# Two groups instead of one by 26 block products, with the weight sums made one group earlier

## The chip, the cores and the metric

The kernel runs on one core of a Trainium2 chip. A core has five engines with their own in-order instruction queues: TensorE (PE in the profile; its weight loads are PEld), VectorE (DVE), ScalarE (ACT), GpSimd (POOL) and SyncE (SP), which here does nothing but issue DMA transfers. [...] All times are device microseconds (us). The metric is the time of one execution on the device; the median of the runs shown is what counts.

## The reference

Two stages follow each other. The first is attention inside chunks of 64 tokens, for 8 batches, 8 heads, 576 tokens and a head size of 64. The second takes its output as `x` of shape (8, 576, 512), mixes it by a Fourier transform over tokens and features, and puts a two-layer perceptron behind it:

```python
mixed = np.real(np.fft.fft(np.fft.fft(x, axis=1), axis=2))
u = x + mixed
un = (u - mean(u)) / np.sqrt(var(u) + 1e-06)
ch = np.maximum(un @ w_ch1, 0.0) @ w_ch2      # 512 -> 2048 -> 512
return u + ch
```

Everything is 32-bit floating point. The two products with `w_ch1` ("up") and `w_ch2` ("down") are by far the largest part.

## The kernel before, in words

**Groups.** The tokens are cut into nine groups of four tiles of 128 tokens, numbered 0 to 8. Groups 0 to 7 belong to one batch each; group 8 holds the middle chunks of all batches. `mlp(g)` runs a group: an up phase, then a down phase. `begin[g]` is the step at which group g starts; a step is one `yield` of these phases, and the other work of the kernel (attention and Fourier mixing of the next batch, weight preparation) is put between the steps by the loop at the end of the kernel. The order on each engine's queue is thus written out by hand: an instruction stands where the loop emits it, and each queue is worked off in that order.

**Three ways to do a down product.** `down_plain` is the direct way. `down_halves` cuts both operands into halves and needs 7 products in place of 8, each of 8 matmuls of 128x128 by 128x256, for two token pairs: 7 x 2 x 8 = 112 matmuls. `down_few` cuts finer and needs 26 products (table `PRODUCTS`, lines 120 to 147), each of 4 such matmuls: 104 matmuls. The price of fewer products is sums. `down_halves` needs sums of activations made by `operands`; `down_few` needs sums of activations made on GpSimd by `sums` (6 in the list `EARLY`, one ahead of the first product, and 21 beside the products), and sums of weight blocks, 23 of them in the list `MADE`. The constant `FEW` (line 1127) says from which group on `down_few` is used: group 8 alone.

**Weights by slab.** From group 1 or 2 on, the weights lie in DRAM, already cut and summed, and come in as slabs through rings. `fetch(1)` loads the slabs of the up phase (256 KB, ring of 10, tile `wa`), `fetch(2)` those of `down_halves` (1 MB, ring of 3, tile `wb`), and `fetch(3)` those of `down_few` (512 KB, tiles `wb`, `xall`, `more`, ring of `NS3` = 11). Each call puts one DMA on SP's queue; that DMA waits until TensorE has read the slab which it overwrites. An up phase has 28 turns of 4 matmuls, one slab each, and a `fetch(1)` behind each turn. In `down_few` there is a `fetch(3)` behind each product.

**Making the weight sums.** `make_rest` (line 1088) is a generator that the loop advances a step at a time, from step `ready_at[NG - 3]` on, which lies four steps into the down phase of group 6. It does the 23 sums of `MADE` in two halves of 128x512 each. For each half it loads eight blocks from DRAM (line 1104), makes the sums on GpSimd (line 1113), and stores the 19 that are wanted to the DRAM tile `s3` (line 1120). Loads and stores go over SP's queue. The list `spare` holds the buffers: 14 pieces of 128x512, taken from tiles that the attention no longer needs. A sum takes a buffer from its front. A store is issued once more than three made sums stand behind it, and its buffer goes back to `spare`; whoever writes to it next waits until that store has landed.

**The order around it.** At step `begin[8] + 2`, two steps into the up phase of group 8, the loop adds five slabs to the ring and issues all eleven `fetch(3)` at once. Each DMA on SP also waits for the DMA issued eight places before it, on SP or ACT, since eight completion semaphores are used in turn. `store` (line 1020) writes finished tiles to the output.

Of the kernel before, what the change touches and what calls it, by code (L numbers as in the profile page):

```python
# [8 lines left out]
FP32 = mybir.dt.float32  # L9
# [7 lines left out]
def kernel(  # L17
# [32 lines left out]
    nc = tc.nc  # L50
# [16 lines left out]
    G = 2 * NM  # L67
# [4 lines left out]
    one_p = ctx.enter_context(tc.tile_pool(name="one", bufs=1))  # L72
    two_p = ctx.enter_context(tc.tile_pool(name="two", bufs=2))
    three_p = ctx.enter_context(tc.tile_pool(name="three", bufs=3))
# [77 lines left out]
        "s24=s10-sb22", "s22=w-s10", "s25=w+s4", "s1=b21-s4", "s17=b21+b41", "s18=b12+b32", "s12=s18-s17", "s6=b42-s18",  # L152
    )
    STORED = tuple(text.split("=")[0] for text in MADE if text[0] == "s")
    NR2, NS3 = len(PRODUCTS), 11
    s3 = dram.tile([len(STORED), 128, Z3], FP32, name="s3")
    slab3 = [wb[:, i * Z3:(i + 1) * Z3].rearrange("p (m e) -> p m e", m=4) for i in range(6)]

# [922 lines left out]
    def block_of(name):  # L1081

        if name[0] == "s":
            return s3[STORED.index(name)]
        o, k = (2, "dw".index(name)) if name in "dw" else ({"b1": 0, "b2": 0, "b3": 4 + "12".index(name[2]), "b4": 4 + "12".index(name[2])}[name[:2]], (int(name[1]) - 1) % 2)
        return s2[o, :, k * Z3:(k + 1) * Z3]

    def make_rest():

        z, spare = Z3 // 2, []
        for i in range(4):
            spare.append(xall[:, 2 * G:2 * G + 4, :].rearrange("p a f -> p (a f)")[:, i * z:(i + 1) * z])
        for tag, n in (("q", 2), ("k", 2), ("zf", 2), ("two", 1), ("qT", 1), ("kT", 1), ("pT", 1)):
            t = one_p.tile([128, n * z], FP32, tag=tag, name="part")
            spare += [t[:, i * z:(i + 1) * z] for i in range(n)]
        last = {x: i for i, text in enumerate(MADE) for x in text.replace("=", "-").replace("+", "-").split("-")}
        for half in range(2):
            part = slice(half * z, (half + 1) * z)  # L1100
            where, behind = {}, []
            for name in ("b31", "b41", "b42", "b11", "b32", "d", "w", "b21"):
                where[name] = spare.pop(0)
                nc.sync.dma_start(out=where[name], in_=block_of(name)[:, part])
                if half and name in ("b41", "b11", "d"):
                    yield
            yield
            for i, text in enumerate(MADE):
                name = text.split("=")[0]
                to = spare.pop(0)  # L1110
                name, *used, op = parsed(text)
                in0, in1 = (where[x] for x in used)
                nc.gpsimd.tensor_tensor(out=to, in0=in0, in1=in1, op=op)
                where[name] = to
                if name in STORED:
                    behind.append(name)
                done_with = [x for x in (*used, name) if last[x] == i]
                while behind and (len(behind) > 3 or i == len(MADE) - 1):
                    old = behind.pop(0)
                    nc.sync.dma_start(out=block_of(old)[:, part], in_=where[old])  # L1120
                    if last[old] <= i and old not in done_with:
                        done_with.append(old)
                spare += [where[x] for x in done_with if x not in behind]
                if i % 2:
                    yield

    FEW = NG - 1
    first_of = {1: 2, 2: 1}
    n_slab = {1: 0, 2: 0, 3: 0}

    def fetch(which):
        i = n_slab[which]
# [276 lines left out]
    with tc.manual_schedule():  # L1409
# [74 lines left out]
        for g in range(NG):  # L1484
            for _ in mlp(g):
# [29 lines left out]
                if t == begin[1] - 1:  # L1515
                    for _ in conv2:
                        pass
                if t == ready_at[NG - 3]:
                    rest_ = make_rest()
                    next(rest_)  # L1520
                if t > ready_at[NG - 3] + 4:
                    next(rest_, None)
                if t == begin[FEW] + 2:
                    more = [xall[:, 2 * G:2 * G + 4, :].rearrange("p a f -> p (a f)")[:, i * Z3:(i + 1) * Z3] for i in range(2)]
                    more += [one_p.tile([128, Z3], FP32, tag=tag, name="more") for tag in ("q", "k", "zf")]
                    slab3.extend(a.rearrange("p (m e) -> p m e", m=4) for a in more)
                    for _ in range(NS3):
                        fetch(3)
                if begin[1] <= t < begin[1] + KF // 2:
                    for _ in range(3):  # L1530
                        next(conv1, None)
# [55 lines left out]
```

## Time and profile before

Three runs of the kernel took 1081.45, 1081.10 and 1078.39 us; the median is 1081.1 us.

| | |
|---|---|
| profiled execution, its own time | 1078.96 us |
| its span, first to last instruction | 1076.9 us |
| granted TensorE clock | 0.998 |
| up phase of group 7 | 875.28 to 925.33 us of the span |
| down phase of group 7 (`down_halves`) | 925.33 to 975.43 us |
| up phase of group 8 | 975.43 to 1026.41 us |
| down phase of group 8 (`down_few`) | 1026.41 to 1071.32 us |

In a row of the profile, "L1377 PE MATMUL dn<-wb,h" is the line of the kernel, the engine, the operation, and the tile written from the tiles read. "<-DVE" names the engine that ended a wait. A line with "SPq" is about SP's queue, which issues DMAs. The chain of work is followed back from the last instruction; in it TensorE's weight loads are counted with its matmuls, so "x8" of a product is 4 matmuls with their 4 loads.

### The profile page before, as it was taken

The numbers are of one execution on the slowest core, as the hardware profiler recorded it, in microseconds if no ns is written. First come the engines' busy times: TensorE is split into PE (matmuls) and PEld (weight loads), VectorE is DVE, ScalarE is ACT, GpSimd is POOL, SyncE is SP. The second block draws the span as 40 slices with busy tenths as digits, with TensorE's granted clock in tenths as the row PEclk, the third lists the DMA queues.
The fourth block names the chain that finished last, engine by engine and source line by source line (L and its number), as shares of the span: only waits on it lengthen the run. The fifth ranks groups of instructions, "written<-read, shape, count | busy, mean of one in ns | idle before, by whom it ended". The sixth has DMA issues, their size and how long they took to land.

```text
span 1076.9 us, 19916 instructions
## 1 busy us (share of the span) xinstructions
PE 1053.0 (98%) x7402; PEld 837.3 (78%) x7402; DVE 585.0 (54%) x1271; ACT 310.3 (29%) x730; POOL 406.1 (38%) x531
## 2 busy tenths in 40 slices
PE   8999989999999999999999999999999999999997
PEld 6645445446888888888888888888888888888786
DVE  4898985324567465664565554745564435433331
ACT  4688563212113411322032312331233012101200
POOL 4311017573515140344134321624061837850281
PEclk9999999999999999999999999999999999999999
DMA  8767466598467546883678256945653569957563
GB/s 176 240 184 214 122 190 210 162 299 292 153 193 224 161 155 181 231 238 118 189 210 229 99 183 199 260 129 189 208 158 110 196 211 317 337 174 241 186 225 107
DMA packets 159293, 212.71 MB, mean 198 GB/s; under 512 B 69308, under 2 KB 106172, under 8 KB 152926
## 3 DMA queue, kind: packets, MB, share of 16 engines
q1 hardware_dynamic: 155548, 208.04, 63.0%
q10 hardware_dynamic: 3330, 2.76, 1.1%
q8 instruction: 59, 0.97, 0.4%
q0 software_dynamic: 320, 0.66, 0.3%
q14 instruction: 36, 0.29, 0.1%
HBM read 177.31 MB, written 34.08 MB: 196 GB/s over the span
## 4 chain that ended last, share of the span: by engine, by line
PE 77%; DMA 6%; DVE 5%; issue 3%; POOL 3%; ACT 3%; SPq 3%; POOLq 0%; DVEq 0%; ACTq 0%
PE pb L1313 18%; PE pa L1262 16%; PE pa L1313 14%; PE pb L1262 12%; PE dn L1377 4%; PE up L1195 2%; PE pt L397 2%; DMA xall<-in_moe_w_ch_dram 2%; PE mix L838 2%; DMA wa<-s 2%; PE z L719 1%; PE xp L498 1%; SPq L263 1%; PE up L1175 1%; PE sc L448 1%
## 5 line engine op out<-in xcount | busy, mean ns | idle before, releaser
L1262 PE MATMUL pa<-unT,wa 128*128 128x256 f32 x672 | 159.9, 381 | 1.6 <-DVE wa L1270 1.6
L1262 PEld LDWEIGHTS pa<-unT,wa 128*128 128x128 f32 x672 | 126.3, 190 | 19.5 <-DVE wa L1270 2.1
L1262 PE MATMUL pb<-wa 128*128 128x256 f32 x448 | 106.7, 381 | 2.6 <-DMA wa<-s 2.6
L1313 PE MATMUL pa<-wb,h 128*128 128x256 f32 x448 | 101.5, 380 | 0.0
L1313 PE MATMUL pb<-wb,h 128*128 128x256 f32 x448 | 100.7, 379 | 0.0
L1262 PEld LDWEIGHTS pb<-wa 128*128 128x128 f32 x448 | 84.2, 190 | 14.8 <-issue 2.8
L1313 PEld LDWEIGHTS pa<-wb,h 128*128 128x128 f32 x448 | 83.9, 190 | 11.3
L1313 PEld LDWEIGHTS pb<-wb,h 128*128 128x128 f32 x448 | 84.1, 190 | 10.9
L1149 POOL TENSOR_TENSOR h<-h 128x256 f32<-128x256 f32 x56 | 47.0, 850 | 96.2 <-DVE wb L1147 93.4
L555 POOL COPY xall<-xall 1x512 f32<-1x512 f32 x28 | 17.8, 636 | 147.9 <-DVE xall L515 120.4
L1268 DVE TENSOR_TENSOR wa<-pb,wa 128x256 f32<-128x256 f32 x56 | 23.7, 424 | 73.0 <-ACT wa L1267 73.0
L1216 PE MATMUL dn<-wb,h 128*128 128x512 f32 x128 | 58.9, 609 | 0.0
L1267 ACT COPY wa<-pa 128x256 f32<-128x256 f32 x56 | 20.8, 372 | 126.8 <-PE pa L1262 126.8
L1195 PE MATMUL up<-unT,wa 128*128 128x512 f32 x128 | 56.8, 596 | 0.0
L1262 PE MATMUL pa<-wa 128*128 128x256 f32 x224 | 53.9, 384 | 0.8 <-DMA wa<-s 0.8
L1262 PE MATMUL pb<-unT,wa 128*128 128x256 f32 x224 | 53.0, 379 | 0.0
L1313 PE MATMUL pb<-wb,yall 128*128 128x256 f32 x224 | 51.2, 382 | 0.0
L1313 PE MATMUL pb<-wb 128*128 128x256 f32 x224 | 50.7, 379 | 0.0
L1313 PE MATMUL pa<-wb,yall 128*128 128x256 f32 x224 | 50.5, 379 | 0.0
L1276 ACT ACTIVATE h<-pa 128x256 f32<-128x256 f32 x56 | 21.5, 383 | 100.7 <-PE pa L1262 99.8
L1175 PE MATMUL up<-unT,wa 128*128 128x512 f32 x108 | 49.4, 598 | 0.0
L1262 PEld LDWEIGHTS pa<-wa 128*128 128x128 f32 x224 | 41.7, 190 | 7.2 <-ACT wa L1267 1.1
(287 smaller groups left out, 1955.7 us busy)
## 6 DMA issues: line engine op xcount, KB each, us to landing
wb<-s SPq DMA_DIRECT2D x49, 1024.0 KB
wa<-s SPq DMA_DIRECT2D x196, 256.0 KB
xall<-in_moe_w_ch_dram SPq DMA_DIRECT2D x22, 512.0 KB
q<-in_q_dram SPq DMA_DIRECT2D x96, 112.0 KB
k<-in_k_dram SPq DMA_DIRECT2D x96, 112.0 KB
wb<-s SPq DMA_DIRECT2D x16, 512.0 KB
v<-in_v_dram SPq DMA_DIRECT2D x124, 64.0 KB
s<-part SPq DMA_DIRECT2D x30, 256.0 KB
```

The lines of the kernel that those rows point to most:

```text
L397: nc.tensor.transpose(pt[:, j, :], src(j), ident)
L838: nc.tensor.matmul(out=mix[:, cols], lhsT=zt[:, T], rhs=tab, start=(T == 0), stop=(T == 3), skip_group_check=True,)
L1149: nc.gpsimd.tensor_tensor(out=h1[:, m, hi], in0=h1[:, m, lo], in1=h1[:, m, hi], op=ALU.subtract)
L1175: nc.tensor.matmul(out=up, lhsT=w1[:, kk, m * 128:(m + 1) * 128], rhs=unT[:, kk], start=(kk == 0), stop=(kk == KD - 1), skip_group_check=True,
L1195: nc.tensor.matmul(out=up, lhsT=w1[:, kk, m * 128:(m + 1) * 128], rhs=unT[:, kk], start=(kk == 0), stop=(kk == KD - 1),)
L1216: nc.tensor.matmul(out=dn, lhsT=h1[:, m, s * 128:(s + 1) * 128], rhs=w2[:, m, :], start=(m == 0), stop=(m == KF - 1),)
L1262: nc.tensor.matmul(out=dst, lhsT=w[:, kk, r], rhs=rhs[o][:, kk], start=(o in (0, 1) and kk == 0), stop=(kk == 1), skip_group_check=True,)
L1267: nc.scalar.copy(a, dst)
L1268: nc.vector.tensor_tensor(out=b, in0=pbs[r][:, 0], in1=a, op=ALU.add)
L1276: nc.scalar.activation(out=h1[:, m, lo], in_=dst, func=ACTF.Relu)
L1313: nc.tensor.matmul(out=dst, lhsT=lhs[:, m], rhs=w[:, m], start=(o in (0, 2) and m == 0), stop=(m == HF - 1), skip_group_check=True,)
L1377: nc.tensor.matmul(out=dst, lhsT=lhs[:, m], rhs=w[:, m], start=(fresh and not half and m == 0), stop=(m == 3), skip_group_check=True,)
```

## The change

`FEW` becomes `NG - 2`, so groups 7 and 8 both run `down_few`; group 7's up phase makes the `EARLY` sums in place of `operands`. For that the weight sums are needed one group earlier, and `make_rest` is rewritten. It has 21 pieces of buffer in place of 14: two each of the tiles `ex` and `pm` and three of `y` are added. It loads 13 of its 16 blocks at once, the other three as buffers come free (`take`). Four of the 23 sums of each half go to VectorE in place of GpSimd: every fourth, unless it reads one of the two sums just before it. The loop advances it at every step without the pause of four steps, and at step `begin[7] + 12` runs what is left of it. There the ring gets two slabs more, eight in all in place of eleven, and two `fetch(3)` are issued in each of the last four steps of group 7's up phase. The slabs of group 8 then follow through the ring behind group 7's products. No DMAs of `fetch(2)` are issued for group 7.

```diff
-    NR2, NS3 = len(PRODUCTS), 11
+    NR2, NS3 = len(PRODUCTS), 8
...
-        for tag, n in (("q", 2), ("k", 2), ("zf", 2), ("two", 1), ("qT", 1), ("kT", 1), ("pT", 1)):
-            t = one_p.tile([128, n * z], FP32, tag=tag, name="part")
+        for pool, tag, n in (
+            (one_p, "q", 2), (one_p, "k", 2), (one_p, "zf", 2), (one_p, "two", 1), (one_p, "qT", 1), (one_p, "kT", 1),
+            (one_p, "pT", 1), (two_p, "ex", 1), (two_p, "ex", 1), (two_p, "pm", 1), (two_p, "pm", 1),
+            (three_p, "y", 1), (three_p, "y", 1), (three_p, "y", 1),
+        ):
+            t = pool.tile([128, n * z], FP32, tag=tag, name="part")
             spare += [t[:, i * z:(i + 1) * z] for i in range(n)]
...
+        def take(keep):
+            while wanted and len(spare) > keep:
+                half, name = wanted.pop(0)
+                places[half][name] = spare.pop(0)
+                nc.sync.dma_start(out=places[half][name], in_=block_of(name)[:, half * z:(half + 1) * z])
+
+        take(8)
+        yield
         for half in range(2):
-            part = slice(half * z, (half + 1) * z)
-            where, behind = {}, []
-            for name in ("b31", "b41", "b42", "b11", "b32", "d", "w", "b21"):
-                where[name] = spare.pop(0)
-                nc.sync.dma_start(out=where[name], in_=block_of(name)[:, part])
-                if half and name in ("b41", "b11", "d"):
-                    yield
-            yield
+            part, where, behind = slice(half * z, (half + 1) * z), places[half], []
             for i, text in enumerate(MADE):
...
-                nc.gpsimd.tensor_tensor(out=to, in0=in0, in1=in1, op=op)
+                eng = nc.vector if i % 4 == 3 and not {MADE[i - 1].split("=")[0], MADE[i - 2].split("=")[0]} & set(used) else nc.gpsimd
+                eng.tensor_tensor(out=to, in0=in0, in1=in1, op=op)
...
                 spare += [where[x] for x in done_with if x not in behind]
+                take(7)
                 if i % 2:
                     yield
-    FEW = NG - 1
+    FEW = NG - 2
...
-                if t == ready_at[NG - 3]:
+                if t == ready_at[FEW - 1]:
                     rest_ = make_rest()
-                    next(rest_)
-                if t > ready_at[NG - 3] + 4:
+                if t >= ready_at[FEW - 1]:
                     next(rest_, None)
-                if t == begin[FEW] + 2:
-                    more = [xall[:, 2 * G:2 * G + 4, :].rearrange("p a f -> p (a f)")[:, i * Z3:(i + 1) * Z3] for i in range(2)]
-                    more += [one_p.tile([128, Z3], FP32, tag=tag, name="more") for tag in ("q", "k", "zf")]
-                    slab3.extend(a.rearrange("p (m e) -> p m e", m=4) for a in more)
-                    for _ in range(NS3):
-                        fetch(3)
+                if t == begin[FEW] + 2 * HF - 4:
+                    for _ in rest_:
+                        pass
+                    slab3.extend(
+                        one_p.tile([128, Z3], FP32, tag=tag, name="more").rearrange("p (m e) -> p m e", m=4)
+                        for tag in ("q", "k")
+                    )
+                if begin[FEW] + 2 * HF - 4 <= t < begin[FEW] + 2 * HF:
+                    fetch(3)
+                    fetch(3)
```

More of the change, by code (lines that the diff above doesn't have):

```diff
@@ L1094, in make_rest @@
             spare.append(xall[:, 2 * G:2 * G + 4, :].rearrange("p a f -> p (a f)")[:, i * z:(i + 1) * z])
-        for tag, n in (("q", 2), ("k", 2), ("zf", 2), ("two", 1), ("qT", 1), ("kT", 1), ("pT", 1)):
-            t = one_p.tile([128, n * z], FP32, tag=tag, name="part")
+        for pool, tag, n in (
[4 more added lines that the diff above has]
+            t = pool.tile([128, n * z], FP32, tag=tag, name="part")
             spare += [t[:, i * z:(i + 1) * z] for i in range(n)]
         last = {x: i for i, text in enumerate(MADE) for x in text.replace("=", "-").replace("+", "-").split("-")}
-        for half in range(2):
-            part = slice(half * z, (half + 1) * z)
-            where, behind = {}, []
-            for name in ("b31", "b41", "b42", "b11", "b32", "d", "w", "b21"):
-                where[name] = spare.pop(0)
-                nc.sync.dma_start(out=where[name], in_=block_of(name)[:, part])
-                if half and name in ("b41", "b11", "d"):
-                    yield
-            yield
+        places = [{}, {}]
+        wanted = [(half, name) for half in range(2) for name in ("b31", "b41", "b42", "b11", "b32", "d", "w", "b21")]
+        def take(keep):
[5 more added lines that the diff above has]
+        yield
+        for half in range(2):
+            part, where, behind = slice(half * z, (half + 1) * z), places[half], []
             for i, text in enumerate(MADE):
-                name = text.split("=")[0]
                 to = spare.pop(0)
```

## The prediction

> **What bounds the kernel now.** The page first: one engine is nearly always busy.
>
> ```profile
> span 1076.9 us, 19916 instructions
> PE 1053.0 (98%) x7402; PEld 837.3 (78%) x7402; DVE 585.0 (54%) x1271; ACT 310.3 (29%) x730; POOL 406.1 (38%) x531
> ```
>
> TensorE is the bound, so I count matmuls and TensorE's gaps in the stages that the change touches. These are the phases of groups 7 and 8, in the busy times by stretch (span, PE, PEld, DVE, ACT, POOL, clock, DMA share, GB/s):
>
> ```profile
> 875.28:925.33 50.05, 49.05 (x226) 42.33 (x225) 24.87 (x52) 13.55 (x31) 34.07 (x29) 1.00 0.89 307
> 925.33:975.43 50.10, 50.10 (x241) 44.14 (x241) 15.80 (x30) 2.45 (x6) 31.29 (x29) 1.00 0.61 204
> 975.43:1026.41 50.98, 48.59 (x225) 42.49 (x225) 16.95 (x40) 13.88 (x31) 7.99 (x7) 1.00 0.61 216
> 1026.41:1071.32 44.91, 44.89 (x208) 39.19 (x207) 12.09 (x30) 0.54 (x2) 26.85 (x22) 1.00 0.58 189
> ```
>
> Rows 1 and 3 (up phases) have idle TensorE time; rows 2 and 4 (down phases) have none. The last row is the form that the change extends: 104 matmuls in 44.91 us, without a gap. The chain of waits gives the cadence, and where the gaps come from:
>
> ```profile
> 980.61 1.74 PE pb L1262 x8
> ...
> 984.16 7.75 DMA wb<-s
> ...
> 991.97 9.89 DMA wa<-s
> ...
> 1002.00 1.97 PE pb L1262 x8
> ```
>
> 4 matmuls take 1.727 us, so one takes 0.432. An up phase is 112 matmuls, 48.36 us; group 8's took 50.98: 2.62 lost, because eleven slabs (5.8 MB) issued at 982.7 to 991 stand ahead of its own weights. Group 7's took 50.05: 1.69 lost. There SP's queue waits for the weight sums, and the sums for buffers (waits of SP's queue, then of GpSimd):
>
> ```profile
> SPq L1120 <- POOL part L1113: 22.6, 16, 5.9
> POOL part L1113 <- DMA s<-part: 23.0, 5, 15.5
> ```
>
> [...] from 984 to 1008 us the DMA share is 0.97 to 1.03 while the weights wait behind the slabs. Saturated 6 us stretches moved 346 to 420 GB/s, most near 380. [...] the 128x256 VectorE sum of line 1148, both inputs in SBUF, took 846 ns on average, that of line 1268 with one input in PSUM 424 ns.
>
> **The change, part by part.**
>
> *Matmuls.* Group 7's down phase goes from 112 to 104: 8 x 0.432 = **-3.45 us**. Its 16 transposes for group 8 (4 x 0.44) stay, so 50.10 becomes 46.65. The last turn of group 8's tiles now has two products (3.45 us) behind it; one 0.69 us copy and four 0.42 us sums on VectorE must end there. They fit.
>
> *The batch of eleven slabs goes.* Group 8's slabs come one by one behind group 7's products: **-2.62 us** in group 8's up phase.
>
> *Activation sums.* Group 7 loses `operands` (16 VectorE sums at 0.69 and 0.85: 12 us; 8 GpSimd sums) and gains 28 GpSimd sums at 1.27, which GpSimd does beside 104 matmuls in group 8 without a TensorE gap. Nothing on the path.
>
> *Sums on VectorE.* 8 x 128x512. The nearest row, line 855, has 0.75 us[...]; I take 8, less than `operands` gave back. Cost nothing, covered by VectorE's idle half; but the evictions of TensorE's results queue behind each, and TensorE behind those. Each sum waits for the store that frees its buffer, so I checked each: the second half's first is due at about 885 with its buffer stored near 884.5, the next at 890 against 888.6, the last two have 7 us or more.
>
> *Slab ring 11 to 8.* A slab is fetched when one product ends and needed 7 products (12.1 us) later; 0.524 MB per 1.727 us is 303 GB/s, below 380. In the trace's own 104-matmul phase the stretches ran at 206 to 315 GB/s with no gap. Nothing, while the ring starts full.
>
> *Weight sums earlier.* This decides. I follow three queues, with these rates: a GpSimd sum 1.27 us; a 256 KB store 4 us from issue to landing (issued 870.4, GpSimd released 875.1; 882.6 to 886.3), 5 where DMA is saturated; one 256 KB transfer per 0.62 to 0.70 us at saturation.
>
> 1. Loads go at 838.3 as now, 13 of them, to 846.5. GpSimd starts at 844.5 instead of 850.5, since its first two sums stand ahead of group 6's output sums. SP's fetches for group 6 wait for TensorE until 846.4 and 853.7; the third, at 861.1, was group 7's and is gone, so four stores go out at 854 to 855.5. GpSimd's next seven sums then end by 867; the trace of before had it idle from 859.6 to 875.1.
> 2. Output stores of group 6 hold SP until 865.0, 868.9, 874.1 and 876.8, as now. The first half's sums end near 882, against 905.
> 3. From 877 on DMA is full. To the end of group 7's up phase SP has 27 stores, 3 loads and 28 `fetch(1)` of 262 KB and 8 slabs of 524 KB: 19.4 MB. The first `fetch(1)` goes at 882.4 (886.05 before). Each has 10 turns from freeing to need, 17 us; I find 5 us or more left for every one. So up 7 has no reason to lose its 1.69 us; as the queue is fuller than before I credit half: **-0.85 us**.
> 4. GpSimd's second half, with the six `EARLY` sums between, is held by buffer stores to about 891.7 and then runs its last 18 instructions back to back: 18 x 1.27 = 22.9, so the last sum ends at 915 and the last store is issued there. `make_rest` is due to be through at step 12 of 16, 911.6; 3 us late.
> 5. The slabs follow from 915.3 at 1.34 us each, with seven `fetch(1)` between. Slab 0 lands near 919.3 (needed at 923.7), slab 4 at 927.4 (930.6), slab 7 at 932.8 (935.8), slab 10 at 937.5 (941). About 3 us to spare; no stall.
>
> *Tail.* The last product ends the same way; 5.6 us stay.
>
> Sum: -3.45 - 2.62 - 0.85 = **-6.9 us**: span 1070.0, the profiled execution 1078.96 - 6.9 = 1072.0. That execution lies 2.1 below the median of the runs (1081.1, which would give 1074.2); I take **1073**.
>
> **The rivals.**
>
> *A: the slabs come late and eat the gain.* By bytes: 19.4 MB from 877 until slab 7 is needed at 935.8 asks for 330 GB/s. At 350 nothing changes. At 300 it takes 64.7 us and the stall is 6 us; down 7 then asks for 303 and does not recover. For it: the up phase of group 7 already had a share of 0.89, at 307 GB/s. Against: that mean holds the waits of SP for sums; the full stretches in it had 358 to 404. Time: 1073 + 6 = 1079, within 0.3% (about what a measurement of this kernel can tell from no change).
>
> *B: the buffer loop runs late, slower than before.* Place: the second half's sums wait in a chain for stores (eight waits, about three sums apart), and SP, in order, has `fetch(1)` and later the slabs behind those stores. Price: each us of landing beyond my 4 to 5 is paid up to eight times in the last sum. A last store at 918 costs nothing, 926 cancels the gain (stall 8), beyond 929 the kernel is over 0.3% slower; that is landing at 6 to 6.5 us. At 931: stall 13, 1073 + 13 = 1086. VectorE's sums, waiting for the same stores, would hold evictions in the same case. For it: before, the second half took 911.1 to 952.6, 1.8 us a sum. Against: 11 us of that were other GpSimd work, and the first half's stores had the fetches of TensorE's pace between them. At that pace, from 883, the end is near 921: stall 3, 1076.
>
> *C: the change does not do what it says.* In the order of the built program group 7's down phase has 104 matmuls and the slabs stand where the text puts them. Left out.
>
> **How the numbers follow.** Likeliest, no stall over 4 us: 0.74, with 1069.5 to 1077. A: 0.12, counted as the same. B beyond its point: 0.14, slower. Faster 0.74, same 0.12, slower 0.14. The range goes from 1068 (all 7.8 us gained, from the lowest run, 1078.39 - 7.8 = 1070.6, less 2.6 for the spread of the runs) to 1083: it leaves out most of B.
>
> **What would show it.** Group 7's down phase at 46.6 us with 104 matmuls of `dn`; group 8's up phase at 48.4 with no wait for `wa`; group 7's up phase at 48.4 to 49.5. Last sum of `make_rest` at 913 to 919 on GpSimd. Wrong if TensorE's first products of group 7's down phase wait for `wb` or `more`, if a `wa` wait of some us stands in its up phase, or if evictions there wait behind a VectorE sum.

## The result: slower by 0.4%, where 0.7% faster was predicted

The changed kernel took 1084.01 us (median of 8 runs, 1082.51 to 1085.91), the kernel before, beside it on the same chip, 1080.72 us (8 runs). The ratio is 1.0036, with a 95% interval of 1.0024 to 1.0048. The prediction was 1073; 1084 lies outside its range as well. The profiled execution took 1082.51 us. Its page, first lines:

```profile
span 1080.5 us, 19943 instructions
PE 1053.7 (98%) x7386; PEld 837.2 (77%) x7386; DVE 593.0 (55%) x1281; ACT 310.1 (29%) x728; POOL 417.3 (39%) x533
```

Eight matmuls are gone (two records each: 7402 to 7386), yet TensorE is busy as long as before. Where the time is shows in the busy times by stretch. These are group 6's down phase, group 7's up and down, group 8's up and down (columns as in the prediction: length, then PE, PEld, DVE, ACT, POOL, clock, DMA share, GB/s):

```profile
822.94:880.17 57.23, 55.28 (x265) 48.40 (x265) 32.91 (x55) 7.85 (x29) 33.93 (x28) 0.97 0.56 188
880.17:932.81 52.64, 50.14 (x225) 43.50 (x224) 22.86 (x45) 13.64 (x31) 39.89 (x31) 0.97 0.88 297
932.81:981.33 48.52, 47.23 (x226) 41.10 (x225) 18.20 (x44) 1.87 (x4) 27.10 (x22) 1.00 0.92 352
981.33:1030.20 48.87, 48.58 (x225) 42.50 (x225) 16.96 (x40) 13.89 (x31) 8.01 (x7) 1.00 0.46 149
1030.20:1075.11 44.91, 44.90 (x209) 39.20 (x207) 12.09 (x30) 0.54 (x2) 26.82 (x22) 1.00 0.66 224
```

Group 6's down phase, whose own products the change does not touch, was this in the kernel before:

```profile
821.87:875.28 53.41, 53.41 (x266) 47.28 (x265) 25.37 (x52) 7.83 (x29) 23.87 (x22) 1.00 0.53 177
```

So the 10.5 us between the predicted span, 1070.0, and 1080.5 come together like this:

| stage | predicted, us | measured, us | more, us |
|---|---|---|---|
| before these phases (the change does nothing there) | 821.87 | 822.94 | 1.07 |
| group 6, down | 53.41 | 57.23 | 3.82 |
| group 7, up (50.05 - 0.85) | 49.20 | 52.64 | 3.44 |
| group 7, down | 46.65 | 48.52 | 1.87 |
| group 8, up | 48.36 | 48.87 | 0.51 |
| group 8, down | 44.91 | 44.91 | 0.00 |
| tail | 5.6 | 5.4 | -0.2 |

Only group 8's two phases came as predicted. The chain of waits in group 8's up phase no longer holds slabs; the load that it still passes costs TensorE 0.3 us there (48.87 less 48.58), not 2.4:

```profile
986.51 1.73 PE pb L1271 x8
...
988.57 10.18 DMA wa<-s
```

TensorE's waits from 840 to 990 us (by line and tile, what ended them, total us, times, longest):

```profile
PE pa L1271 <- DVE h L1287: 2.5, 1, 2.5
PE pt L397 <- DVE un L994: 1.9, 1, 1.9
PE dn L1386 <- DMA more<-s: 1.3, 1, 1.3
```

These are 5.7 us. Behind each of the first two the clock was halved for 3.413 us, which costs 1.7 us each time. Three stretches around the wait that ended at 869.2 us show it in the clock's column (third from the end): 1.00 in the stretch with the wait, 0.50 in the next, in which TensorE was busy throughout and has 9 matmul records, and 1.00 again in the third, with 17. The last section has the other such stretches.

```profile
866.66:870.08 3.42, 1.48 (x9) 1.05 (x8) 2.94 (x4) 0.00 (x0) 3.34 (x3) 1.00 0.00 0
870.08:873.49 3.41, 3.41 (x9) 2.71 (x9) 0.96 (x3) 0.00 (x0) 0.13 (x1) 0.50 0.31 79
873.49:876.90 3.41, 3.41 (x17) 2.98 (x16) 2.13 (x6) 0.00 (x0) 0.00 (x0) 1.00 0.71 166
```

**Why the normalised tile was late.** VectorE's queue in group 6's down phase, changed kernel (start, us, line, operation):

```profile
862.48 0.97 DVE L1015 TENSOR_TENSOR wa<-unT 128x256 f32<-128x256 f32 x1
863.48 1.38 DVE L1016 TENSOR_TENSOR wa<-unT,wa 128x256 f32<-128x256 f32 x1
864.78 1.48 DVE L1017 TENSOR_TENSOR unT<-unT 128x256 f32<-128x256 f32 x1
866.19 1.48 DVE L1018 TENSOR_TENSOR wa<-unT,wa 128x256 f32<-128x256 f32 x1
867.60 1.48 DVE L994 TENSOR_SCALAR un<-xall,st,rstd 128x512 f32<-128x512 f32 x1
869.00 0.41 DVE L1339 TENSOR_TENSOR wb<-pb,wb 128x256 f32<-128x256 f32 x1
...
873.82 0.42 DVE L1016 TENSOR_TENSOR wa<-unT,wa 128x256 f32<-128x256 f32 x1
```

The same instructions in the kernel before:

```profile
861.86 0.42 DVE L1016 TENSOR_TENSOR wa<-unT,wa 128x256 f32<-128x256 f32 x1
862.20 0.42 DVE L1017 TENSOR_TENSOR unT<-unT 128x256 f32<-128x256 f32 x1
862.54 0.42 DVE L1018 TENSOR_TENSOR wa<-unT,wa 128x256 f32<-128x256 f32 x1
862.87 0.54 DVE L994 TENSOR_SCALAR un<-xall,st,rstd 128x512 f32<-128x512 f32 x1
864.59 0.42 DVE L1330 TENSOR_TENSOR wb<-pb,wb 128x256 f32<-128x256 f32 x1 [1.18 <-PE pb L1313]
```

Of the first five, all but line 1015 take 1.4 to 1.5 us in place of 0.4 to 0.5, so 0.9 to 1.1 us longer, beside GpSimd sums of 1.27 us each. In the changed kernel GpSimd sums weights back to back from 857.9 to 870.2; in the kernel before it was idle from 859.6 to 875.1. The changed kernel has its own comparison: at 873.8 us, with GpSimd idle, line 1016 takes 0.42 us again. Counted from the start of the phase, the tile of line 994 is ready at 46.1 us in place of 41.5, and TensorE waits 1.95 us for it.

**Why the weight sums were late.** A sum on GpSimd ended at 863.2 (first line); it was stored from SyncE's queue at 871.2, 8 us later, and the sum that needs its buffer began at 880.3, 9 us after that. GpSimd's queue, then SyncE's, then what SyncE had waited for from 855 to 882 us:

```profile
861.88 1.29 POOL L1121 TENSOR_TENSOR xall<-part 128x512 f32<-128x512 f32 x1
...
880.31 1.27 POOL L1121 TENSOR_TENSOR xall<-part 128x512 f32<-128x512 f32 x1 [10.10 <-DMA s<-xall]
```

```profile
869.43 1.10 SPq L1027 DMA_DIRECT2D out_dram<-wb  x2
870.63 0.46 SPq L1128 DMA_DIRECT2D s<-part  x1
871.18 2.03 SPq L1128 DMA_DIRECT2D s<-xall  x1
```

```profile
SPq L1027 <- DVE wb L1339: 11.5, 1, 11.5
```

SyncE stood 11.5 us at an output store of group 6 (line 1027), with the weight stores behind it. Until 865.6 it stood there for TensorE's product, and from then to 869.4 for VectorE, whose last sum for that tile (line 1339, at 869.00) had to go behind the five slowed instructions. In the kernel before, that sum (line 1330, at 864.59) followed its product at once.

Then the landing. In the trace each of these weight stores has 16 counts on its semaphore. Of the store issued at 871.2, 14 came by 877.5 and the last two at 878.8 and 880.2; the sum began at 880.3. Two output stores of the LO kind stood ahead of it, issued at 869.4 and 870.0.

GpSimd's waits for such stores came to 10.1 and 6.1 us, both in the first half of the weight sums. That half ended at 893.1; the prediction had 882. The second half had no further wait for a store and kept the delay: its last sum ended at 926.4, and the first slab was issued at 926.8; the prediction had 915 and 915.3.

### The profile page after: what moved, and what is told of

It reads as the page before. It is cut to its first block, busy times and chain, and to the rows that moved or that the text cites. A ratio compares the mean times of both kernels' runs of the same rounds, so it can differ in the third digit from the quotient of the medians.

```text
span 1080.5 us, 19943 instructions
## 1 busy us (share of the span) xinstructions
PE 1053.7 (98%) x7386; PEld 837.2 (77%) x7386; DVE 593.0 (55%) x1281; ACT 310.1 (29%) x728; POOL 417.3 (39%) x533
## 4 chain that ended last, share of the span: by engine, by line
PE 74%; DMA 8%; DVE 5%; issue 4%; POOL 3%; ACT 3%; SPq 2%; DVEq 0%; POOLq 0%; ACTq 0%
PE pa L1271 16%; PE pb L1322 15%; PE pb L1271 12%; PE pa L1322 12%; PE dn L1386 7%; PE up L1204 2%; PE pt L397 2%; DMA xall<-in_moe_w_ch_dram 2%; DMA v<-in_v_dram 2%; PE mix L838 2%; PE z L719 1%; DMA wa<-s 1%; PE xp L498 1%; SPq L263 1%; PE up L1184 1%
## 5 line engine op out<-in xcount | busy, mean ns | idle before, releaser
L1271 PEld LDWEIGHTS pb<-wa 128*128 128x128 f32 x448 | 84.4, 190 | 11.5
L1322 PE MATMUL pa<-wb,h 128*128 128x256 f32 x384 | 87.2, 380 | 0.0
L1322 PE MATMUL pb<-wb,h 128*128 128x256 f32 x384 | 86.8, 381 | 0.0
L1322 PEld LDWEIGHTS pb<-wb,h 128*128 128x128 f32 x384 | 72.5, 191 | 9.5
L1322 PEld LDWEIGHTS pa<-wb,h 128*128 128x128 f32 x384 | 71.8, 190 | 9.7
L1158 POOL TENSOR_TENSOR h<-h 128x256 f32<-128x256 f32 x48 | 40.6, 855 | 93.6 <-DVE wb L1156 91.2
L1172 POOL TENSOR_TENSOR h<-h 128x512 f32<-128x512 f32 x36 | 45.1, 1267 | 27.2 <-ACT h L1291 22.5
L1386 PE MATMUL dn<-wb,h 128*128 128x256 f32 x224 | 50.5, 379 | 0.0
L855 POOL TENSOR_TENSOR xall<-y,xall 128x513 f32<-128x513 f32 x14 | 21.4, 1526 | 68.3 <-DVE y L849 68.3
```

The costliest lines, as they stand in the source:

```text
L1158: nc.gpsimd.tensor_tensor(out=h1[:, m, hi], in0=h1[:, m, lo], in1=h1[:, m, hi], op=ALU.subtract)
L1172: nc.gpsimd.tensor_tensor(out=out_, in0=a, in1=b, op=op)
L1271: nc.tensor.matmul(out=dst, lhsT=w[:, kk, r], rhs=rhs[o][:, kk], start=(o in (0, 1) and kk == 0), stop=(kk == 1), skip_group_check=True,)
L1322: nc.tensor.matmul(out=dst, lhsT=lhs[:, m], rhs=w[:, m], start=(o in (0, 2) and m == 0), stop=(m == HF - 1), skip_group_check=True,)
L1386: nc.tensor.matmul(out=dst, lhsT=lhs[:, m], rhs=w[:, m], start=(fresh and not half and m == 0), stop=(m == 3), skip_group_check=True,)
```

## Experiments

Each ratio is to the kernel before, run beside it. The edits are made to the changed kernel, or to the one named. Executions of one kernel spread over some 5 us, so single profiles are read for waits, and medians and ratios for time.

**Is it the sums, or the products?** The first run leaves out the weight sums with their loads and stores; the products then read other blocks that lie in DRAM, so its results are not those of the reference.

```diff
-            return s3[STORED.index(name)]
+            o = STORED.index(name)
+            return s2[o % 7, :, o // 7 % 2 * Z3:(o // 7 % 2 + 1) * Z3]
...
-                if t == ready_at[FEW - 1]:
-                    rest_ = make_rest()
...
```

> The changed kernel without `make_rest`: none of the 46 sums, their 16 loads and 38 stores; the slabs of the 26 products are read from blocks that lie in DRAM anyway, so the products are of the wrong weights. Two groups of 26 products and the ring of eight stay. Theory V (only the making of the sums costs): both gaps and the wait for the slabs go, 1080.7 - 3.45 - 2.6 - 1.7 = 1073. A rival P (26 products beside group 8's preparation, or a ring of eight, cost time themselves): above 1076.

1072.13 us, ratio 0.9922 (0.9894 to 0.9950), from five executions of 1071.7 to 1078.5 us. The profiled one is the slowest; it lost its time ahead of these phases. The phases themselves, group 7 up and down:

```profile
882.59:930.93 48.34, 48.34 (x225) 42.55 (x224) 16.96 (x40) 13.71 (x31) 7.83 (x7) 1.00 0.62 194
930.93:977.59 46.66, 46.66 (x226) 41.09 (x225) 18.56 (x44) 1.87 (x4) 27.13 (x22) 1.00 0.94 335
```

There is no idle TensorE time in them, nor in group 8's up phase, which took 48.34 us. The products, the ring and the missing batch of slabs are worth what was predicted; what is lost is lost through the weight sums, their loads and stores included. The counterpart keeps the sums where they are and gives group 7 its old down phase:

```diff
-    FEW = NG - 2
+    FEW = NG - 1
...
-                if t == ready_at[FEW - 1]:
+                if t == ready_at[FEW - 2]:
...
```

> The changed kernel with 26 products in group 8 alone: the weight sums are made early and with the new buffers as in the changed kernel, group 7 has its 112 matmuls, and the eight slabs are issued in the last four steps of group 8's up phase. Theory V: it pays for the gap in group 6's down phase (3.7) and for a VectorE sum's wait in group 7's up phase (up to 4.2), and gains 2.6 in group 8's up phase, where no batch of eleven slabs stands in the way: 1082 to 1086. Rival P: 1080.7 - 2.6 = 1078.

1089.17 us, ratio 1.0078 (1.0053 to 1.0102): 8.4 us slower than the kernel before, and more than the 1082 to 1086 expected. So the early sums cost time with no new product to be late for. The 8.4 us are not their price in the changed kernel, though: here group 7's up phase still makes `operands` beside them and waits 5.8 us in the profile, and group 8's up phase gains its 2.6 us.

**VectorE's share.**

```diff
-                eng = nc.vector if i % 4 == 3 and not {MADE[i - 1].split("=")[0], MADE[i - 2].split("=")[0]} & set(used) else nc.gpsimd
+                eng = nc.gpsimd
```

> The changed kernel with all 46 weight sums on GpSimd, none on VectorE. Theory V: the wait of 3.4 us of a VectorE sum for a buffer's store in group 7's up phase, and TensorE's gap of 2.5 us behind it with its 1.7 us of slow clock, are gone (-4.2); but GpSimd has eight sums more (8 x 1.27), the last sum ends some 5 us later and TensorE waits about 4 us more for the first slabs of group 7's down phase: 1082 to 1085, with the gap moved. Rival D: -0 in the up phase, +5 at the slabs: 1088.

1087.18 us, ratio 1.0055 (1.0034 to 1.0076): worse, above the 1082 to 1085 expected and near the 1088 of the rival. TensorE's waits:

```profile
PE dn L1386 <- DMA wb<-s: 6.4, 1, 6.4
PE pt L397 <- DVE un L994: 2.1, 1, 2.1
```

The wait for the normalised tile is there without any weight sum on VectorE, so it comes from GpSimd's sums. And the wait in the up phase, gone here, came back as a wait of 6.4 us for slabs, not of 4: GpSimd's last sum ended at 930.0.

**The normalised tile.** In `down_halves` the normalisations go ahead of the operand sums of `combined` (lines 1015 to 1018), so that TensorE's next tile does not stand behind them.

```diff
-                        if k == 5 + 2 * j and j >= 2:
+                    for j in range(2, G):
+                        if k == 5 + 2 * j:
```

> The changed kernel, with the normalising of the next group's tile (VectorE) emitted ahead of that group's four operand sums in `down_halves`. Theory V (VectorE is held by GpSimd's sums[...], the normalised tile of group 7 comes late, TensorE waits 1.95 us, and the clock then runs at half speed for 3.41 us, which costs 1.71): the gap near 868 us goes, group 6's down phase is back at 53.4 us, and the time falls by about 3.7 us to 1080.3. Rival D (the DMA engines are full and everything later is set by them): the down phase gets shorter but the first products of group 7 wait longer for their slabs; 1083 to 1084 stays.

1081.30 us, ratio 1.0012 (0.9999 to 1.0024), 2.6 us less than the change. TensorE's waits from 840 to 990 us:

```profile
PE pa L1271 <- DVE h L1287: 3.1, 1, 3.1
PE pa L1271 <- ACT wa L1276: 1.5, 1, 1.5
```

The wait at line 397 is gone and nothing took its place in group 6, whose down phase takes 53.5 us again. Its half clock is gone too, so 3.8 us are gained there, and part of it is lost in group 7's up phase, where the waits are 4.6 us and not 2.5. The rival, that the DMA engines set everything, asked for 1083 to 1084 us and a longer wait for the first slabs, which the list does not have. The first wait left is an eviction behind a weight sum on VectorE, which waits for a GpSimd sum, which waits for a stored buffer.

**What a wait costs.** The kernel before, with 11 idle additions on VectorE ahead of the same normalisation:

```diff
+                            if g == 6 and j == 3:
+                                for _ in range(11):
+                                    nc.vector.tensor_tensor(out=warm, in0=warm, in1=warm, op=ALU.add)
```

> The kernel before with 11 additions on a tile that nothing reads (about 0.46 us each) ahead of the last normalisation of group 6's down phase, so that VectorE is late there as in the changed kernel. Theory (a gap of some 2 us in TensorE's work is what group 6's down phase cost): 2 us slower than before if the gap alone counts, 3.7 if the clock is halved for 3.4 us after it as in the changed kernel's profile. Rival (other work hides it): no change.

1085.25 against 1081.21 us, ratio 1.0039 (1.0025 to 1.0054): 4.2 us. Its profile has a wait of 2.7 us there and no half clock behind it:

```profile
PE pt L397 <- DVE un L994: 2.7, 1, 2.7
```

The lower end of the interval, 2.7, is the wait alone. Half clock in other executions does not explain the rest: the granted clock is on record for each, and its mean is 0.9967 in the 11 executions of this kernel and 0.9967 in the 20 of the kernel before. What the rest is stays open.

**Landing: the output stores on ScalarE.** On top of the run with the normalisations first; then the same edit on the kernel before.

```diff
-                nc.sync.dma_start(out=to, in_=o[r0:r0 + CH])
+                nc.scalar.dma_start(out=to, in_=o[r0:r0 + CH])
```

> The change with the normalisations ahead of the combined products, and the output stores of the LO kind issued from ScalarE instead of SyncE. Theory (the buffer stores of the weight sums land 7 to 9 us after issue because they queue behind the output stores[...]): they land in 3 to 4 us now, GpSimd's waits of 9.6 and 5.4 us at its sums shrink below 3 each, VectorE's wait of 4.0 us at line 1121 and TensorE's gaps of 3.1 and 1.5 us in group 7's up phase go, with the stretch at half clock; about 1077 us. Rival (the landing is set by the load on the engines, not by the queue): waits and gaps stay, about 1081 us.

> The kernel before with only the LO output stores on ScalarE's queue. Both theories: it has no early weight sums that wait for stores near an output store, so about 1080.5 us, at most 1.5 us faster[...]. It prices that edit alone, so that the run beside it is read rightly.

1089.26 us, ratio 1.0069 (1.0046 to 1.0093), and 1085.86 us, ratio 1.0042 (1.0021 to 1.0064). The edit itself costs 4.6 us, which neither theory had. The second run's profile shows most of it lost in the first groups: a matmul at 168 us of the span comes 1.6 us later than the same one in the kernel before, one at 210 us 6.9 later. An issue took ScalarE 0.5 us at the median there. So the first run's time tells little of its question. What its profile does tell is that GpSimd still waited 9.8 us for a store: a queue of its own for the LO stores did not bring the buffers back in 4 us. Without VectorE's sums in the second half:

```diff
-                eng = nc.vector if i % 4 == 3 and not {...
+                eng = nc.vector if half == 0 and i % 4 == 3 and not {...
```

> The run with normalisations first and LO stores on ScalarE, and VectorE's share of the weight sums kept to the first half; the second half's go to GpSimd. If VectorE's wait for a stored buffer is what still holds TensorE in group 7's up phase, that gap goes, and GpSimd's last sum ends some 5 us later: 1076 to 1078 us while the slabs still come in time; with the slabs late by up to 3 us, 1080.

1089.55 us, ratio 1.0075 (1.0055 to 1.0094). The wait behind the weight sum went, 4.9 us of slab waits came, and 3.4 for a copy on ScalarE: missed.

**Landing: stores moved or left out.** On top of the run with the normalisations first, two stores of group 6 are held back, or left out.

```diff
-                    store(low, olow)
+                    if g == FEW - 1:
+                        held.append((low, olow))
+                    else:
+                        store(low, olow)
...
+                if t - begin[FEW] in (5, 9):
+                    store(*held.pop(0))
```

> The change with the normalisations first, and group 6's two LO output stores, which nothing waits for before group 7's down phase, issued 6 and 10 steps into group 7's up phase (some 19 and 31 us in) and not at 868 and 878 us. Theory (the weight sums' buffers come back late[...]): the first store lands in 4 to 5 us and not 9, GpSimd's first wait falls from 9.6 to under 5 us, VectorE's sum near 892 us no longer waits, TensorE's gaps of 3.1 and 1.5 us and the half clock go: about 1076 us. Rival (the landing is late whatever the output stores do): as with the normalisations first alone, 1081 us.

> The change with the normalisations first, and group 6's LO output stores left out, so two tiles of that group are never written to the output; all else is computed. It is the bound of moving them: by the theory every weight store of the first half lands in 4 to 5 us, GpSimd's waits of 9.6 and 5.4 us together fall below 5, and TensorE's gaps in group 7's up phase go: 1074 to 1077 us. By the rival, 1081 us with the same waits.

These texts name the stores wrongly: `low` is the first two of the group's four tiles, one of the LO and one of the HI kind. 1083.86 us, ratio 1.0024 (1.0012 to 1.0035), and with the two left out 1079.01 us, ratio 0.9981 (0.9968 to 0.9994); 1076, and 1074 to 1077, were expected. The landing did change: in the second run the 16 counts of a weight store came between 867.3 and 868.0, and those of the next between 868.7 and 868.8. But GpSimd's wait did not; SyncE's and GpSimd's waits of that run:

```profile
SPq L1027 <- DVE wb L1347: 9.1, 1, 9.1
```

```profile
POOL part L1121 <- DVE h L1290: 11.7, 1, 11.7
```

SyncE now stood 9.1 us at the third tile's output store. (The second row's name misleads: by its semaphore that sum waited for a weight store, issued at 878.1, 8.5 us after its data was ready and just behind the third tile's LO store; its last two counts came at 886.0 and 886.7. VectorE's instruction happened to end then.) So of these 17 us half is landing and half is the queue, and the queue became the next suspect.

**The queue.** Again with the normalisations first: all of group 6's output stores on ScalarE, in this group alone:

```diff
-                nc.sync.dma_start(out=to, in_=o[r0:r0 + CH])
+                (nc.scalar if n in groups[FEW - 1] else nc.sync).dma_start(out=to, in_=o[r0:r0 + CH])
...
-                    eng = nc.scalar if r else nc.sync
+                    eng = nc.scalar if r or n in groups[FEW - 1] else nc.sync
```

> The change with the normalisations first, and all of group 6's output stores (of that group alone) issued from ScalarE. Theory (in SyncE's queue the weight sums' stores stand behind output stores that wait for TensorE's evictions, so a buffer whose sum was done at 870 is stored only at 882): the weight stores are issued within 1 us of their sums, GpSimd's waits of 9.6 and 5.4 us fall below 5 together, VectorE's wait of 4.0 us near 892 and TensorE's gap of 3.1 us behind it go: 1075 to 1078 us; ScalarE's eight issues, some 0.5 us each, may cost up to 1.5 us at the head of group 7. Rival (the landing alone is late): waits and time as with the normalisations first alone, 1081 us.

1083.20 us, ratio 1.0030 (1.0018 to 1.0042). GpSimd's waits for stores fell from 15.0 to 7.8 us and VectorE's went, but TensorE lost 5.5 us to ScalarE, more than the 1.5 allowed for:

```profile
PE pa L1271 <- ACT wa L1276: 5.5, 1, 5.5
```

Then SyncE's output stores of group 6 held back to the first four steps of group 7:

```diff
+        hold = n in groups[FEW - 1] and not now
+        if hold:
+            held.append((n, o))
...
+                if begin[FEW] < t <= begin[FEW] + 4:
+                    store(*held.pop(0), now=True)
```

> The same aim on SyncE's own queue: group 6's output stores that SyncE issues are held back to the first four steps of group 7's up phase (about 881 to 893 us), when their data has long been there, so that nothing waits behind them. By the queue theory the sums run on without a wait up to about 881, GpSimd's last sum ends near 915 and no gap follows in group 7's up phase: 1074 to 1077 us. By the landing theory the four stores only move the late landings some 10 us on: 1080 us or more.

1078.71 us, ratio 0.9982 (0.9965 to 1.0000): 5.8 us less than the change, and short of the 1074 to 1077 expected. GpSimd's waits, then all of TensorE's from 840 to 990 us:

```profile
POOL xall L1130 <- DMA s<-xall: 4.2, 1, 4.2
POOL part L1130 <- DMA s<-part: 3.8, 3, 1.6
```

```profile
PE dn L1396 <- DMA wb<-s: 4.2, 1, 4.2
```

From the first weight sum to the end of the last it took 73.3 us, against 80.1 in the changed kernel and 70.5 in the prediction. SyncE still stood 6.3 us, to 880.0, now at a weight store whose own sum is one of VectorE's and went behind the four sums of `combined`, each slowed to 1.3 to 1.5 us. So holding the output stores back does not empty the queue of everything that waits. No wait is left in group 7's up phase but the one at its end, for the first slab. The clock is at half for 6.8 us from 930.9 on; 1.9 us of that lie in the wait itself, so 2.5 us are lost (16 matmul records took 6.12 us there and 3.62 at full clock; group 7's down phase takes 49.16 us, not 46.65). The held stores without the other edit:

> The changed kernel with group 6's output stores held back and nothing else altered: the edit that is worth 2.6 us on top of the normalisations first, here by itself. If the two causes add, 1084.0 - 2.6 = 1081.4 us, and TensorE's gap at the turning of the normalised tile (1.95 us in the changed kernel) stays or grows, since GpSimd runs on beside VectorE; if the queue in SyncE was behind that gap too, it goes and the time is 1079 us.

1079.30 us, ratio 0.9987 (0.9975 to 0.9999), 5.3 us less than the change. That is the time expected if the wait for the normalised tile went with the queue, but the wait is still there. The two causes do not add: 2.6 and 5.3 singly, 5.8 together. In this profile the wait for the tile comes without a half clock (the granted clock is 1.00 over 800 to 1070 us and 0.999 over all):

```profile
PE dn L1395 <- DMA wb<-s: 2.2, 2, 1.9
PE pt L397 <- DVE un L994: 2.0, 1, 2.0
PE dn L1395 <- DMA more<-s: 1.2, 1, 1.2
```

**The slabs.** On top of both edits: two slabs loaded early, then six between the weight stores, then the same with the last two at the end of the phase.

```diff
-                if begin[FEW] + 2 * HF - 4 <= t < begin[FEW] + 2 * HF:
+                if t == begin[FEW] + 2 * HF - 7 or begin[FEW] + 2 * HF - 4 <= t < begin[FEW] + 2 * HF - 1:
```

> The normalisations first, group 6's output stores held back, and the first two slabs of group 7's down phase (stored blocks that no weight sum makes) loaded five steps earlier, ahead of the last weight stores in SyncE's queue. If the slabs behind the last stores are what TensorE's 4.2 us at the head of that down phase waits for, that gap goes, with the half clock behind it: 1078.7 - 4.2 = 1074.5 us, or down to 1073 in runs that lost the clock too. If the third slab is as late, 1077 to 1078 us.

> The normalisations first, group 6's output stores held back, and the first six slabs of group 7's down phase loaded between the last weight stores, each some five stores after its own block was stored, and not behind all of them. If the slabs' place in SyncE's queue is the third cause, TensorE's wait of 2.7 us for the third slab and the 6.8 us at half clock behind it (3.4 us lost) go: 1079.0 - 2.7 - 3.4 = 1073 us, the predicted time; 1075 to 1076 if only some runs lost the clock before. If another load is late in its place, 1077 to 1079 us.

> As the run with six slabs early, but the seventh and eighth (into the two buffers that the last weight sums were in) loaded at the end of the up phase and not 3 steps before it, so that SyncE doesn't stand 6.6 us at 928 to 936 waiting for the last weight stores with seven loads behind it. If that standing is what made that run 3 us slower than the one with two slabs early: 1074 to 1077 us, no wait of TensorE for a slab over 1 us. If the loads are late in any order because GpSimd's last sum ends at 923 to 925 us, 1079 us again.

1079.01 us (ratio 0.9983, 0.9971 to 0.9995), 1082.11 (1.0017, 1.0004 to 1.0031) and 1079.57 (0.9999, 0.9986 to 1.0013). Expected were 1074.5, 1073 and 1074 to 1077 us, or up to 1079 where another load would be late; the second is above even that. Each took one wait away and got another: 2.7 us for the third slab; 3.8 and 1.9 for later ones, because SyncE stood 6.6 us for a weight store before it could load the seventh; and in the last:

```profile
PE dn L1399 <- DMA more<-s: 2.8, 1, 2.8
```

That tile is a buffer of the last weight sums. The order of the loads alone does not cure it.

## Why the prediction was wrong

**Right.** *Matmuls*, *The batch of eleven slabs goes* and *Tail*: without the sums the kernel takes 1072.13 us for the 1073 predicted, and group 8's up phase lost its batch. *Slab ring 11 to 8*: without the sums, group 7's down phase ran on the ring of eight in 46.66 us without a wait. *Activation sums* cost nothing on the path: group 7's up phase took 48.34 us there.

**Wrong: the price of GpSimd's sums to VectorE.** *Weight sums earlier*, step 1, was right that GpSimd's next sums run on where it had been idle (to 870.2). It priced this at nothing. The prediction had the longer time from the kernel before (846 ns for a VectorE sum with both inputs in SBUF, 424 for one with an input in PSUM), and *Sums on VectorE* priced the eight new sums alone, at an estimate of 8 us together. The instructions that paid were those already there: five of VectorE's in a row, 0.4 to 0.5 us each, took 0.97 to 1.48. The wait of 1.95 us and the 1.7 us of half clock behind it are all but 0.2 of the 3.82 us of group 6's down phase in the profile; putting the tile out of the way gave back 2.6 us of median.

**Wrong: the 4 us of a store.** This rate, on which steps 1 to 4 rest, was misread from the trace of before. The prediction took "issued 870.4, GpSimd released 875.1" for one store:

```profile
865.04 1.10 SPq L1027 DMA_DIRECT2D out_dram<-wb  x2
866.24 0.44 SPq L1120 DMA_DIRECT2D s<-part  x1
...
870.40 0.84 SPq L1120 DMA_DIRECT2D s<-part  x1
```

```profile
875.14 1.27 POOL L1113 TENSOR_TENSOR part<-xall 128x512 f32<-128x512 f32 x1 [15.53 <-DMA s<-part]
```

By the trace's semaphores the sum at 875.14 waited for the store of 866.24, whose last count came at 875.07: 8.8 us. The store of 870.40 landed at 879.6, after 9.2. The second pair is wrong in the same way: the sum at 886.3 waited for a store issued at 875.7, 10.5 us, and the store issued at 882.6 took 7.0. Four to 5 us hold further on in that trace (3.7 to 5.3 for the weight stores issued from 885.6 to 902.4), where no LO store stands just ahead. So the kernel before had the slow landings already; the 8.7 and 9.0 us of the changed kernel's stores at 870.6 and 871.2 are nothing new. The prediction's own rival B set its point at a landing of 6 to 6.5 us.

**Wrong: step 2.** It let the output stores hold SyncE "as now", until 865.0, 868.9, 874.1 and 876.8. They held it until 869.4, 873.5, 879.4 and 882.3, of which 1.1 us is the trace's own lateness. For the first, the tile's last sum on VectorE stood behind the slowed instructions; for the others TensorE itself was late by then. So the first cause feeds the second, which is one reason why they do not add. The time that counts runs from the end of a sum to its buffer's return: 17.1 us for the one followed above, 8.0 in the queue and 9.1 landing. Holding the output stores back gave 5.3 us.

For the landing the traces give the counts, and no cause. Of a LO store three count events are in the trace, one about 1 us after the issue and two at the end (870.4, then 874.7 and 874.8 for the one issued at 869.4), where the weight stores have sixteen. Of a weight store just behind two LO stores two counts are late: in the kernel before (874.0 and 875.1 of the store issued at 866.2, whose other fourteen came by 871.0), in the changed one (878.8 and 880.2, against 877.5), and with the LO stores on ScalarE's queue (888.4 and 888.5, over 1.4 us behind the others, of the store that SyncE issued at 881.9). Where the stores ahead were left out, the two weight stores in their place had all their counts within 0.7 us; a single count late by 1.4 us stands elsewhere in that run too (the store issued at 862.4), so a late count comes without a LO store ahead too. Why the last two counts behind LO stores come late was not shown.

**Wrong: steps 4 and 5, by 11 us.** The last sum ended at 926.4, not 915; the 11 us were lost by the end of the first half (893.1, not 882). "VectorE's sums, waiting for the same stores, would hold evictions in the same case" was written under rival B and given 0.14; group 7's up phase shows it (2.5 us and the half clock), with the difference that VectorE's sum waited for one of GpSimd's, which had waited 6.1 us for a store. B's mechanism was thus right, and its point from which it decides, a last sum at 929, nearly so. Its place was not: two long waits at the end of the first half, not eight in the second. Nor was its stall, 8 us for an end at 926, since TensorE's other waits, in series, had already made it late for the slabs: 1.3 us were left to wait for. That is also why taking one wait away gives little: the slabs are behind it. Without the first two causes, the wait for the slabs is 4.2 us, 6.7 with the clock; the 6.5 us between the ratios 0.9982 and 0.9922 are about that. Rival A, the bytes, is not tested by itself; group 7's down phase moved 352 GB/s where the ring asks for 303.

**Missing: the clock.** No step priced a halved clock behind a wait. It took 3.4 of the 10.5 us in the profiled execution. For the medians the granted clocks of all executions allow an estimate (1 less the clock, times the span): 4.7 us lost on average in the 8 of the changed kernel, 3.1 in the 25 of the kernel before that ran beside the first four experiments, so up to some 1.6 of the 3.9 us that the change is slower (a half clock inside a wait costs nothing, and each clock is given to 0.001, 1.1 us). Step 3's 0.85 us for group 7's up phase did not come either, for the waits above.

What stays open: whether earlier sums, which need the buffers of the attention before they are free, would bring the rest, and whether the sums on GpSimd alone would do so once the output stores are held back. Neither was tried. The best versions found, held stores with or without the normalisations first, are 0.1 to 0.2% faster than the kernel before, at the edge of what these runs can tell.

## What to carry to other kernels

Before a latency is taken from a trace, make sure that the transfer and the instruction that it is said to release share a semaphore; the next release after an issue may belong to an earlier transfer. Before work is moved under another engine's cover, list what else runs on both engines in those microseconds: here the moved GpSimd sums slowed instructions of VectorE that the change never touched. When a buffer loop goes through a shared in-order DMA queue, count from the end of the producer to the buffer's return, with every store ahead of it that waits for someone else. And when several things are late for one deadline, repairing one shows the next: measure the bound with all of them gone (here by leaving the sums out) before working on any.

## What the runs showed of the hardware

Up to TensorE's last matmul, the profile of the kernel before has one half-clock stretch and that of the changed kernel three, all 3.413 us long. In both profiles the clock's records at full speed are whole multiples of that length (the changed kernel's 153.600, 706.559, 23.893 and 177.493 us are 45, 207, 7 and 52 times 3.413, the other's 153.600 and 914.772 us 45 and 268 times). Divided at the clock's changes and at every 3.413 us between them, the two profiles have these stretches at full clock with 1.6 us or more of idle TensorE time:

| profile | stretch, us | TensorE idle in it, us | clock in the next one |
|---|---|---|---|
| changed kernel | 893.97 to 897.38 | 2.50 | 0.50 |
| changed kernel | 156.69 to 160.10 | 2.06 | 0.50 |
| kernel before | 154.99 to 158.41 | 2.05 | 0.50 |
| changed kernel | 866.66 to 870.08 | 1.94 | 0.50 |
| kernel before | 998.08 to 1001.49 | 1.89 | 1.00 |
| kernel before | 8.22 to 11.64 | 1.69 | 1.00 |
| changed kernel | 44.05 to 47.46 | 1.61 | 1.00 |
| kernel before | 42.35 to 45.77 | 1.60 | 1.00 |

So a wait's price depended on where it fell. The changed kernel's wait of 1.95 us lay in one stretch, as shown with the result, and cost 3.7 us with its half clock. The longer one of the run with the idle additions, 2.7 us, lay in two (1.64 and 1.04 us idle), and in that run the second of them was at full clock:

```profile
866.32:869.74 3.42, 1.78 (x9) 1.22 (x7) 3.18 (x8) 0.00 (x0) 0.00 (x0) 1.00 0.21 89
869.74:873.15 3.41, 2.37 (x13) 2.19 (x14) 1.92 (x4) 0.00 (x0) 0.00 (x0) 1.00 0.05 10
```

Counted from the first instruction, the first border on record comes at 4.8 us in the profile of the kernel before and at 6.5 us in that of the changed kernel. An estimate from the rows above: a wait of about 2 us on the path costs 2 us, or 3.7 where a half-clock stretch follows.
